# A second key table made on chip for the half units, presets of block one moved to weight places, and the second pair's loads issued later

## The chip, the cores and the metric

The kernel runs on one NeuronCore of a Trainium2 chip, in one launch. The metric is the device time of that core in microseconds (us); lower is better. The core has TensorE (PE, with its weight loads shown apart as PEld), VectorE (DVE), ScalarE (ACT), GpSimd (POOL) and SyncE (SP), which issues nearly all DMAs here.

## The reference

A linear attention with a decaying state, then two feed-forward layers one after the other. Batch 4, 8 heads, 768 steps, head width 48; so 3072 tokens of width 384, and a hidden width of 2048.

```python
for t in range(S):                       # attention, per batch and head
    cur = einsum('bhd,bhe->bhde', u * k[t], v[t])
    y[t] = einsum('bhd,bhde->bhe', r[t], state + cur)
    state = w * state + einsum('bhd,bhe->bhde', k[t], v[t])
x = y reshaped to (3072, 384)
h = x @ w_in;  x = (max(h, 0) + alpha * min(h, 0)) @ w_out        # layer A
h = x @ w_in2; x = (h * tanh(softplus(h))) @ w_out2               # layer B
```

## The kernel before

The sequence is cut into six blocks of 128 steps. A block holds all four batches. In block one each **unit** is one batch with its 128 steps (units 0 to 3, `B` = 4). From block two on a unit is half of a block's steps (64) of two batches ("half unit", units 4 to 23); two half units in a row make a **pair**, which shares one load of r and k. Inside a unit the recurrence is turned into matrix products: r and k are scaled by powers of the decay w (`prep_rk`, `prep_pair`, with the table `RK`), `scores` multiplies them (L337), a triangular mask copies the scores over a **preset** diagonal (`preset` on ACT, L319; `masked` on DVE, L341), and the result meets v (`attend0` L353, `batch` L369 and L390). The state `T` is updated from k times v (`states_first` L415, inside `batch` L383), with k scaled by a second table, `Kn`, whose row is the step and whose column is the feature (`prep_kn`, a multiplication on POOL, L310).

`Kn` comes from the inverse powers in `RK`: four ACT copies scale it by a power of w into a scratch tile (L251), four PE transposes turn it into the bank `acc2` (L252), two ACT copies bring it to SBUF (L255). That is written for 128 steps. The half units need the upper 64 rows of the table in both halves of the partitions, so `half_Kn` overwrites the lower half with the upper one by a DMA on SP's queue (L259), and `half_tables` makes the matching half identity and half mask on POOL (L177, L179). Both stand in the plan at the place -94.44, behind the multiplications of units 0 to 3, which need the full table.

After the attention of a block, layer A runs over its 512 tokens: 16 **slots** per block, one for each 128 columns of the hidden width. A slot multiplies x with a weight tile (`mA_h`, L156), applies the activation (ACT `m` L485, DVE `g` L487), splits the result into a high and a low part (ACT L82, DVE L85), and multiplies with the second half of the weight tile (`mA_out`, L517). In block one each weight tile f is also made just before its slot: a raw load (L102), two ACT scalings (L108, L109), a DVE join into `wj` (L114), a high part (ACT L82, or POOL L125 for odd f from 3 on) and a low part (DVE L85). Slot numbers start at 0 and run on; layer B follows when all of A is done.

The order of the work is written by hand. `at(place, work)` puts a piece of work at a place; all pieces are sorted by place, and the engines get them in that order. Places below -90 are the start, before slot 0; the dictionary `E` holds them by name. Each engine then works through its own list in order, so an instruction that waits holds up all that stand behind it on that engine. Loads stand in SP's list in the same way. A load also waits until one of eight completion slots is free, so that some eight loads of SP are under way at most.

Before any planned work SP gets the loads of units 0 to 3, the weights f = 0 to 2, both r and k loads of the first pair and the inputs of units 4 and 5, then f = 3, then `load_unit(B + 2)`: the eight r and k loads of the second pair (units 6 and 7) and the two of unit 6's r, k, v rows (`nat`); then f = 4 to 6. Weights f = 7 and on follow from the plan (at 0.4 and later). Tiles named `w8` to `w15` hold the inputs of units 0 to 3 until the weights with those numbers need the room; `wraw` has three buffers for raw weights. The preset tiles `A` (512 columns of fp32 for each of two halves) have two buffers in the attention's pool, for full and half units alike.

Of the kernel before, what the change touches and what calls it, by code (L numbers as in the profile page):

```python
# [36 lines left out]
PR = 112  # L37
# [26 lines left out]
def attention_and_two_ff(ctx: ExitStack, tc, rkT, nat, wT, ub, consts, w1, w2, alphaT, out):  # L64
    nc = tc.nc
    act, dve, pool, pe, dma = nc.scalar, nc.vector, nc.gpsimd, nc.tensor, nc.sync
    per = ctx.enter_context(tc.tile_pool(name="per", bufs=1))
# [114 lines left out]
    def by_seat(out, in_, *lead, by=(dma, dma)):  # L182

        for q, h, rows in ((0, 0, (0, 64, 0)), (1, 1, (48, 112, 48)), (0, 1, (0, 48, 64)), (1, 0, (64, 112, 0))):
            a, b, o = rows
            by[h].dma_start(out=out[(slice(o, o + b - a),) + lead + (slice(2 * q, 2 * q + 2),)],
                          in_=in_[(slice(a, b),) + lead + (slice(2 * h, 2 * h + 2),)])

    def load_unit(u):
        if u < B:  # L190
            f = NF - 2 * B + 2 * u
            rk = per.tile([PR, 2, NPR, C], F32, tag=f"w{f}", name=f"w{f}u")
            n = per.tile([128, 4, DM], F32, tag=f"w{f + 1}", name=f"w{f + 1}u")
            by_seat(rk, rkT[u], slice(None))
            dma.dma_start(out=n[:, 1:3], in_=nat[u, :, 1:3])
            inp[u] = (rk, n, n[:, 2])
            vz_t[u] = n[:, 3].rearrange("s (q c e) -> s q c e", q=2, c=KC)
            return
        j, bp, half = seat_of_unit(u)
        if half == 0:  # L200
            rk_t[j, bp] = [att.tile([PR, 2, NPR, C], F32, tag="rk", name="rk", bufs=4) for _ in range(2)]
            for i in range(2):
                by_seat(rk_t[j, bp][i], rkT[B * j + 2 * bp + i], slice(None))
        n = att.tile([128, 3, DM], F32, tag="nat", name="nat", bufs=3)
        for i in range(2):
            dma.dma_start(out=n[HALF[i]], in_=nat[B * j + 2 * bp + i, HALF[half]])
        inp[u] = (rk_t[j, bp], n, n[:, 2])

    RK = att.tile([PR, 2, NPR, C], F32, name="RK")
    uw = att.tile([PR, NPR, 2], F32, name="uw")  # L210
    w64 = att.tile([PR, NPR], F32, name="w64")
    w96 = att.tile([PR, NPR], F32, name="w96")
    Kn = att.tile([128, NPR, 2, D], F32, name="Kn")
    T = att.tile([PR, B, NPR, 64], F32, name="T")
    def tables():

# [27 lines left out]
        dve.tensor_copy(w64, sq[:, 1])  # L244
        mul(uw, uw, wide(wt, 2))

    def table_Kn():
        kw = new("m")[0:PR].rearrange("d (p s) -> d p s", p=NPR)
        t = bank("acc2")
        for p in range(NPR):  # L250
            act.activation(out=kw[:, p, :], in_=RK[:, 1, p, :], func=AF.Copy, scale=w96[:, p:p + 1])  # L251
            pe.transpose(t[:, p * C:p * C + PR], kw[:, p, :], ident[:PR, :PR])  # L252
        tv = t.rearrange("s (q r x) -> s q r x", q=2, r=2)
        for h, rows in enumerate(ROWS):
            act.activation(out=Kn[:, 2 * h:2 * h + 2].rearrange("s r q d -> s q r d"), in_=tv[:, :, :, rows], func=AF.Copy)  # L255

    def half_Kn():

        dma.dma_start(out=Kn[HALF[0]], in_=Kn[HALF[1]])  # L259

    w_stage = {0: "w4", 1: "w5", 2: "w6", 3: "w7", 7: "w9", 8: "w11", 9: "w13", 10: "w15"}

# [5 lines left out]
    A_t = {}  # L268
# [38 lines left out]

    def prep_kn(u):
        n = inp[u][1]
        pool.tensor_tensor(out=n[:, 1], in0=n[:, 1], in1=Kn.rearrange("s p a d -> s (p a d)"), op=ALU.mult)  # L310

    def preset(u, h):

        if h == 0:
            t = att.tile([128, 2, NPR, C], F32, tag="A", name="A", bufs=2)
            A_t[u] = t if u < B else t[:, 0].rearrange("s p t -> s (p t)").rearrange("s (h p t) -> s h p t", h=2, p=NPR)
        for j in range(NPR):
            p, q = HEAD[h, j]
            act.activation(out=A_t[u][:, h, j, :], in_=ident if u < B else id2, func=AF.Copy, scale=c_t[u][1][:, 2 * p + q, :])  # L319
# [324 lines left out]


    LAG = 2
    E = dict(warm=[-101.3, -99.45, -98.6, -98.1, -97.8, -96.05, -95.8, -93.45, -95.1, -94.8], Kn=[-97.9], rk=[-101.95, -100, -97.6, -95.7], c=[-100.45, -99.35, -96.95, -95.65], sc=[-99.7, -98.25, -96.5, -95.55], pad=[-99.95, -99.9, -97.75, -97], p=[-99.95, -99.2, -96.85, -95.6], m=[-98.95, -97, -96.2, -95.05], a=[-98.5, -96.05, -95.9, -94.95], hi=[-97.65, -95.4, -95.85, -94.65], lo=[-95.65, -94.15, -94.85, -94], kn=[-97.7, -96.05, -95.5, -94.45], st=[-95.3, 0.95], w=[-98.85, -96.4, -96, -95.25, -95, -94.85, -93.9, -93.9, -94.4, -0.5, 0.6, 0.85], u4=[-95.6, -94.95, 0.15, 0.1, 0.65, -94.35], u5=[0.2, 0.2, 2.25], half=[-94.44], p4=[-93.8, -93.7], m4=[0.75, 0.85])
    K = dict(scale=1.8, join=1.25, hi=1, lo=0.67, g=0.55, ghi=0.8, glo=1.1, t=1.25, x=0.7, pre0=0.65, pre1=0.7, m0=-0.25, m1=-0.9, c=-0.89, r0=-1.6, r1=-0.6, kn=0.7, c2=0.15)
    POOL_HI = range(3, NF, 2)
    AT = {B: 2} | {u: 4 * u - 15 for u in range(B + 1, NU)}  # L650
# [5 lines left out]
    def more_raw(upto):  # L656
        while w_next[0] < min(upto, NF):
            n = w_next[0]
            load_raw(0, n, w_stage.get(n, "wraw"))
            w_next[0] += 1  # L660
# [4 lines left out]
    def at(place, work, *args):  # L665
        plan.append((place, len(plan), work, args))
# [49 lines left out]
    with tc.manual_schedule():  # L716
# [3 lines left out]
        for h, i in HEAD:  # L720
            if i < 3 and i != 1:
                act.dma_start(out=uw[ROWS[h], i:i + 2, h],
                              in_=ub[0].rearrange("(h r q d) -> h q d r", h=2, r=2, q=2)[h, i // 2])
# [10 lines left out]
        more_raw(3)  # L734
        load_unit(B + 1)
        more_raw(4)
        load_unit(B + 2)
        more_raw(7)
        pool.memset(zz, 0.0)
        keep_warm(30)  # L740
# [2 lines left out]
        pool.memset(T, 0.0)  # L743
        tables()
        at(-100.5, dve.tensor_scalar, oma, al, -1.0, 1.0, ALU.mult, ALU.add)
        at(E["Kn"][0], table_Kn)
        for place in E["warm"]:
            at(place, keep_warm, 3)
        for u in range(B):
            for work, name in ((prep_rk, "rk"), (c_first, "c"), (pad_v, "pad"), (scores, "sc"),  # L750
                               (attend0, "a"), (x_first, "hi"), (x_first_lo, "lo")):
                at(E[name][u], work, u)
            for q in range(2):
                at(E["p"][u] + 0.01 * q, preset, u, q)
                at(E["m"][u] + 0.01 * q, masked, u, q)
            at(E["kn"][u], prep_kn, u)
        at(E["half"][0], half_Kn)
        at(E["half"][0], half_tables)
        at(E["st"][0], states_first, 0)
        at(E["st"][1], states_first, 2)  # L760
        for f in range(3):
# [18 lines left out]
        for f in range(NF):  # L780
            s = 16 + 4 * f
# [18 lines left out]
        for n in range(0, NB + LAG_B, 2):  # L800
# [7 lines left out]
            for m in pair:  # L808
# [78 lines left out]
```

## Time and profile before

| what | value |
|---|---|
| runs of the kernel before | 1450.11, 913.66, 916.17 us; median 916.17 us |
| the profiled execution, its own time | 912.67 us |
| its span in the profile | 910.9 us, so 1.8 us lie around it |
| mean granted TensorE clock | 0.984 of full speed |
| busy in the span | PE 97%, PEld 84%, DVE 70%, ACT 68%, POOL 10% |
| chain of work that ended last | PE 86%, DVE 3%, ACT 2% of the span |

The profile is of one execution. Engines' shares are of the whole span; the parts of the span differ, and the rows below are therefore cut to stretches. Times in rows are us from the span's start. A row of the timeline gives the start, the length, the engine, the line, the operation, and in brackets how long the engine had stood idle and what ended that. Matmuls overlap, so that the length of several together is not the sum. The clock column of a window is the granted TensorE clock, 1.00 for 2.4 GHz and 0.50 for 1.2 GHz.

### The profile page before, as it was taken

Reading aid. Unit: us, or ns where it says so; the run is one execution under the profiler, and the core shown is the slowest. Engines: PE = TensorE matmul, PEld = TensorE weight load, DVE = VectorE, ACT = ScalarE, POOL = GpSimd, SP = SyncE. Lnnn points to the kernel's source line nnn. Section 1 sums busy time; section 2 is a strip of 40 time slices with the busy share of each in tenths; the row PEclk is TensorE's granted clock in tenths of the full one; section 3 lists DMA queues with packets and bytes.
Section 4 is the critical chain, followed back from the end, with each engine's and each line's share of the span. In section 5 each row is a group of like instructions: output and inputs, shape, how many; then the busy total and the mean of one; then the engine's idle time right before and its main releaser. Section 6 shows DMA issues by size and latency. Waiting matters only on the chain.

```text
span 910.9 us, 17108 instructions
## 1 busy us (share of the span) xinstructions
PE 883.9 (97%) x6684; PEld 761.3 (84%) x6684; DVE 636.3 (70%) x1025; ACT 623.2 (68%) x1193; POOL 90.2 (10%) x112
## 2 busy tenths in 40 slices
PE   9859999999999999999999999999999999999998
PEld 8747878887887887888888898998999999989997
DVE  5639876565665665644565687787787787787876
ACT  4746744554444544454454798898898898898985
POOL 1322231211112111110001100000000000000000
PEclk9879999999999999999999999999999999999999
DMA  7974433435434444311442200200100200100000
GB/s 224 235 271 148 135 103 123 136 108 155 144 113 130 149 138 145 128 63 62 162 133 69 105 1 1 70 1 1 70 1 0 70 1 1 36 1 1 35 1 35
DMA packets 34672, 79.79 MB, mean 88 GB/s; under 512 B 5728, under 2 KB 21792, under 8 KB 34592
## 3 DMA queue, kind: packets, MB, share of 16 engines
q1 hardware_dynamic: 34000, 78.70, 27.8%
q8 instruction: 52, 0.85, 0.4%
q14 instruction: 28, 0.23, 0.1%
q10 hardware_dynamic: 592, 0.00, 0.0%
HBM read 60.89 MB, written 15.73 MB: 84 GB/s over the span
## 4 chain that ended last, share of the span: by engine, by line
PE 86%; DVE 3%; ACT 2%; issue 1%; DMA 1%; POOL 0%; SPq 0%; DVEq 0%; ACTq 0%; POOLq 0%
PE h L156 40%; PE acc L517 20%; PE acc L625 10%; PE sc L625 7%; PE yt L625 3%; PE sc L337 1%; PE sc L383 1%; PE yt L390 1%; PE h L369 1%; DVE rk L280 1%; PE yt L369 1%; DMA x<-y 1%; POOL w L125 0%; SPq L458 0%; ACT ghi L82 0%
## 5 line engine op out<-in xcount | busy, mean ns | idle before, releaser
L156 PE MATMUL h<-x,w 128*128 128x512 f32 x1728 | 419.7, 392 | 6.2 <-DMA x<-y 2.7
L156 PEld LDWEIGHTS h<-x,w 128*128 128x128 f32 x1728 | 323.4, 188 | 76.1 <-issue 5.6
L517 PE MATMUL acc<-ghi,w 128*128 128x512 f32 x516 | 178.1, 399 | 0.0
L485 ACT ACTIVATE m<-h 128x512 f32<-128x512 f32 x96 | 57.3, 597 | 105.0 <-PE h L156 105.0
L517 PEld LDWEIGHTS acc<-ghi,w 128*128 128x128 f32 x516 | 98.5, 191 | 22.4
L487 DVE SCALAR_TENSOR_TENSOR g<-m,oma,h 128x512 f32<-128x512 f32 x96 | 71.5, 745 | 64.2 <-ACT m L485 63.9
L82 ACT ACTIVATE ghi<-g 128x512 fp32r<-128x512 f32 x86 | 54.3, 631 | 77.4 <-PE acc L517 55.3
L517 PE MATMUL acc<-glo,w 128*128 128x512 f32 x258 | 102.2, 396 | 0.0
L85 DVE TENSOR_TENSOR glo<-g,ghi 128x512 fp32r<-128x512 f32 x86 | 60.8, 707 | 57.7 <-ACT ghi L82 57.7
L625 PE MATMUL acc<-w,ghiB 128*128 128x384 f32 x384 | 98.0, 336 | 0.0
L573 DVE SCALAR_TENSOR_TENSOR a<-ghi,h 128x512 f32<-128x512 f32 x96 | 66.0, 687 | 36.1 <-ACT ghi L570 28.6
L573 DVE SCALAR_TENSOR_TENSOR g<-s,c 128x512 f32<-128x512 f32 x96 | 66.3, 690 | 22.0 <-ACT s L570 19.0
L82 ACT ACTIVATE ghiB<-g 128x512 fp32r<-128x512 f32 x106 | 65.8, 621 | 18.5 <-DVE g L573 8.0
L85 DVE TENSOR_TENSOR gloB<-g,ghiB 128x512 fp32r<-128x512 f32 x106 | 72.6, 685 | 7.8 <-ACT ghiB L82 7.8
L581 ACT ACTIVATE m<-h 128x512 f32<-128x512 f32 x96 | 56.0, 584 | 27.9 <-PE h L156 27.9
L570 ACT ACTIVATE ghi<-m,half 128x512 f32<-128x512 f32 x96 | 69.6, 725 | 3.2
L625 PEld LDWEIGHTS acc<-w,ghiB 128*128 128x128 f32 x384 | 69.7, 188 | 1.3
L570 ACT ACTIVATE glo<-ghi,m 128x512 f32<-128x512 f32 x96 | 68.0, 708 | 0.1
L570 ACT ACTIVATE s<-s,m 128x512 f32<-128x512 f32 x96 | 68.0, 709 | 0.0
L570 ACT ACTIVATE s<-glo,m 128x512 f32<-128x512 f32 x96 | 68.0, 709 | 0.0
L573 DVE SCALAR_TENSOR_TENSOR b<-ghi,a 128x512 f32<-128x512 f32 x96 | 67.4, 702 | 0.1
L573 DVE SCALAR_TENSOR_TENSOR c<-glo,b 128x512 f32<-128x512 f32 x96 | 65.7, 684 | 0.0
(174 smaller groups left out, 1193.7 us busy)
## 6 DMA issues: line engine op xcount, KB each, us to landing
wrawr<-in_w SPq DMA_DIRECT2D x24, 768.0 KB, 4.6
nat<-in_nat SPq DMA_DIRECT2D x40, 288.0 KB, 4.3
w2d<-wj SPq DMA_DIRECT2D x16, 384.0 KB, 2.7
wraw<-w2d SPq DMA_DIRECT2D x16, 384.0 KB, 3.0
rk<-in_rkT SPq DMA_DIRECT2D x40, 128.0 KB, 3.0
x2d<-xo SPq DMA_DIRECT2D x6, 768.0 KB, 4.0
x<-x2d SPq DMA_DIRECT2D x6, 768.0 KB, 4.3
out<-oo SPq DMA_DIRECT2D x24, 192.0 KB, 1.9
```

The source lines that it names most:

```text
L82: act.activation(out=hi, in_=src, func=AF.Copy)
L85: eng.tensor_tensor(out=lo, in0=src, in1=hi.bitcast(F32), op=ALU.subtract)
L156: pe.matmul(h, w_in(layer, f, a, c), x[:, b, c, :], start=(k == 0), stop=(k == 3 * KC - 1))
L280: dve.tensor_tensor(out=rk, in0=rk, in1=w.unsqueeze(2).to_broadcast([PR, 2 * NPR, 2, HC]), op=ALU.mult)
L369: pe.matmul(y[i][64 * q:64 * q + 64, p * HC:(p + 1) * HC], T[ROWS[h], 2 * bp + i, k, :], pair[i][ROWS[h], 0, k, t], start=(r == 0 and not ...
L485: act.activation(out=m, in_=hA[s], func=AF.Relu, scale=-1.0)
L487: dve.scalar_tensor_tensor(out=g, in0=m, scalar=oma[:, f:f + 1], in1=hA.pop(s), op0=ALU.mult, op1=ALU.add)
L517: pe.matmul(acc[0][c], w_out(0, f, a)[:, c * 128:(c + 1) * 128], g[b], start=(f == 0 and k == 0), stop=(f == NF - 1 and k == 2))
L570: act.activation(out=out, in_=in_, func=AF.Square, scale=scale, bias=fin[bias])
L573: dve.scalar_tensor_tensor(out=out, in0=in0, scalar=scalar, in1=in1, op0=op0, op1=ALU.mult)
L581: act.activation(out=bnew("t", n), in_=v["h", n], func=AF.Tanh, scale=0.5)
L625: pe.matmul(acc[1][t][:, :DM], g[a][:, t * C:(t + 1) * C], w_out(1, f, b), start=(f == 0 and k == 0), stop=(f == NF - 1 and k == 2))
```

## The change

Three things are done.

- `Kn` gets a leading index of two. `table_Kn(0)` makes the full table at place -97.9 as before; `table_Kn(1)` makes one for the half units at -95.25: the four scaling copies read the upper 64 steps twice, so that the transposes leave them in both halves of the partitions. `prep_kn` takes table 1 for half units. `half_Kn` and its DMA go. In `E`, `Kn=[-97.9]` becomes `Kn=[-97.9, -95.25]`; no other place in it changes.
- The preset tiles of block one lie in the places of the weight tiles f = 2 and 3; the half units' presets have their own tile `Ah`, half as large, in two buffers.
- `load_unit(B + 2)` moves from the list written ahead of the plan to the plan, at place 1.5.

```diff
-    Kn = att.tile([128, NPR, 2, D], F32, name="Kn")
+    Kn = att.tile([128, 2, NPR, 2, D], F32, name="Kn")
...
-    def table_Kn():
+    def table_Kn(i):
+
         kw = new("m")[0:PR].rearrange("d (p s) -> d p s", p=NPR)
         t = bank("acc2")
         for p in range(NPR):
-            act.activation(out=kw[:, p, :], in_=RK[:, 1, p, :], func=AF.Copy, scale=w96[:, p:p + 1])
+            if i:
+                act.activation(out=kw[:, p, :].rearrange("d (h s) -> d h s", h=2), func=AF.Copy, scale=w96[:, p:p + 1],
+                               in_=RK[:, 1, p, HC:].unsqueeze(1).to_broadcast([PR, 2, HC]))
+            else:
+                act.activation(out=kw[:, p, :], in_=RK[:, 1, p, :], func=AF.Copy, scale=w96[:, p:p + 1])
             pe.transpose(t[:, p * C:p * C + PR], kw[:, p, :], ident[:PR, :PR])
         tv = t.rearrange("s (q r x) -> s q r x", q=2, r=2)
         for h, rows in enumerate(ROWS):
-            act.activation(out=Kn[:, 2 * h:2 * h + 2].rearrange("s r q d -> s q r d"), in_=tv[:, :, :, rows], func=AF.Copy)
-
-    def half_Kn():
-
-        dma.dma_start(out=Kn[HALF[0]], in_=Kn[HALF[1]])
+            act.activation(out=Kn[:, i, 2 * h:2 * h + 2].rearrange("s r q d -> s q r d"), in_=tv[:, :, :, rows], func=AF.Copy)
...
-        pool.tensor_tensor(out=n[:, 1], in0=n[:, 1], in1=Kn.rearrange("s p a d -> s (p a d)"), op=ALU.mult)
+        pool.tensor_tensor(out=n[:, 1], in0=n[:, 1], in1=Kn[:, u >= B].rearrange("s p a d -> s (p a d)"), op=ALU.mult)
...
-            t = att.tile([128, 2, NPR, C], F32, tag="A", name="A", bufs=2)
-            A_t[u] = t if u < B else t[:, 0].rearrange("s p t -> s (p t)").rearrange("s (h p t) -> s h p t", h=2, p=NPR)
+            A_t[u] = (per.tile([128, 2, NPR, C], F32, tag=f"w{2 + u % 2}", name="A") if u < B
+                      else att.tile([128, 2, NPR, HC], F32, tag="Ah", name="Ah", bufs=2))
...
-        load_unit(B + 2)
...
-        at(E["Kn"][0], table_Kn)
+        for i in range(2):
+            at(E["Kn"][i], table_Kn, i)
...
-        at(E["half"][0], half_Kn)
         at(E["half"][0], half_tables)
+        at(1.5, load_unit, B + 2)
```

On ACT, near the end of block one's attention, the list of the kernel before has the copies of the first state `T` and then the scalings of weight f = 1 (`w5r`):

```order
L82 ACTIVATE x<-acc_295 128x3x128
L417 ACTIVATE T<-acc_490 48x8x48 x2
L108 ACTIVATE w5r<-w5r 128x768
L109 ACTIVATE w5r<-w5r 128x768
L82 ACTIVATE x<-h 128x3x128
```

In the changed kernel the same place reads:

```order
L82 ACTIVATE x<-acc_282 128x3x128
L418 ACTIVATE T<-acc_477 48x8x48 x2
L253 ACTIVATE m<-RK,w_97 112x128 x4
L260 ACTIVATE Kn<-acc_497 128x2x2x48 x2
L108 ACTIVATE w5r<-w5r 128x768
L109 ACTIVATE w5r<-w5r 128x768
L82 ACTIVATE x<-h 128x3x128
```

Six ACT instructions have come in ahead of weight f = 1 and of the split of unit 3's result. On PE the same step puts four transposes between the states of units 0 and 1 (L415 before, L416 after) and the product of unit 3 (L353, L354). PE of the kernel before:

```order
L415 MATMUL acc_490<-w9u 48x48 x8
L415 MATMUL acc_490<-w11u 48x48 x8
L469 MATMUL acc_510<-ghi 128x128 x3
L353 MATMUL h<-A,w15u 64x128 x6
L353 MATMUL h<-A,w15u 48x128 x6
```

PE of the changed kernel:

```order
L416 MATMUL acc_477<-w9u 48x48 x8
L416 MATMUL acc_477<-w11u 48x48 x8
L257 MATMUL acc_497<-cst,m 128x112 x4
L470 MATMUL acc_509<-ghi 128x128 x3
L354 MATMUL h<-A,w15u 64x128 x6
L354 MATMUL h<-A,w15u 48x128 x6
```

The transposes stand ahead of unit 3's product; the L469 (L470) matmuls are ones on zeros that keep TensorE busy. On SP, from the raw load of f = 2 (`w6r`) on, the kernel before has:

```order
L102 DMA w6r<-in_w 128x1536
L206 DMA nat<-in_nat 64x1152 x2
L102 DMA w7r<-in_w 128x1536
L186 DMA rk<-in_rkT 64x2x256 x2
L186 DMA rk<-in_rkT 48x2x256 x2
L186 DMA rk<-in_rkT 64x2x256 x2
L186 DMA rk<-in_rkT 48x2x256 x2
L206 DMA nat<-in_nat 64x1152 x2
L102 DMA wrawr<-in_w 128x1536 x3
L259 DMA Kn<-Kn 64x384
L102 DMA w9r<-in_w 128x1536
L102 DMA w11r<-in_w 128x1536
```

The changed kernel has there:

```order
L102 DMA w6r<-in_w 128x1536
L206 DMA nat<-in_nat 64x1152 x2
L102 DMA w7r<-in_w 128x1536
L102 DMA wrawr<-in_w 128x1536 x3
L102 DMA w9r<-in_w 128x1536
L102 DMA w11r<-in_w 128x1536
L186 DMA rk<-in_rkT 64x2x256 x2
L186 DMA rk<-in_rkT 48x2x256 x2
L186 DMA rk<-in_rkT 64x2x256 x2
L186 DMA rk<-in_rkT 48x2x256 x2
L206 DMA nat<-in_nat 64x1152 x2
L102 DMA w13r<-in_w 128x1536
```

The second pair's ten loads stand behind the raw weights f = 4 to 8 instead of ahead of them, and the table's copy is gone. The lists of POOL and DVE keep their order.

## Rows read from the trace of the kernel before

**Rows 1.** Page, part 1: busy time, share of the span and instructions.
```profile
PE 883.9 (97%) x6684; PEld 761.3 (84%) x6684; DVE 636.3 (70%) x1025; ACT 623.2 (68%) x1193; POOL 90.2 (10%) x112
```
**Rows 2.** Waits, 40 to 85 us: who waited for whom, total, times, longest.
```profile
POOL nat L310 <- DMA Kn<-Kn: 17.1, 1, 17.1
```
**Rows 3.** Timeline, 45 to 63 us, the first half unit's batch (slots 0 to 2).
```profile
45.20 0.51 SPq L259 DMA_DIRECT2D Kn<-Kn  x1
...
52.47 0.58 ACT L485 ACTIVATE m<-h 128x512 f32<-128x512 f32 x1
56.01 0.99 POOL L310 TENSOR_TENSOR nat<-nat,Kn 128x384 f32<-128x384 f32 x1 [17.10 <-DMA Kn<-Kn]
...
57.06 1.11 PE L383 MATMUL sc<-nat 64*64 64x48 f32 x32 [6.68 <-POOL nat L310]
...
60.04 0.83 POOL L125 CAST w<-wj 128x768 fp32r<-128x768 f32 x1
...
61.78 0.74 DVE L487 SCALAR_TENSOR_TENSOR g<-m,oma,h 128x512 f32<-128x512 f32 x1
...
62.46 0.79 PE L517 MATMUL acc<-ghi,w 128*128 128x512 f32 x1
```
**Rows 4.** Windows: stretch, length, busy PE, PEld, DVE, ACT, POOL; clock; DMA share; GB/s.
```profile
50.39:60.97 10.58, 1.11 (x32) 0.95 (x32) 1.05 (x3) 3.19 (x7) 4.75 (x6) 0.62 0.87 336
64.15:67.36 3.21, 3.21 (x10) 2.50 (x10) 0.87 (x2) 0.83 (x3) 0.00 (x0) 0.63 0.97 255
84.36:99.30 14.94, 14.94 (x84) 12.13 (x86) 12.67 (x18) 10.02 (x15) 4.61 (x4) 1.00 0.50 143
61.78:79.02 17.24, 15.83 (x100) 12.20 (x91) 14.36 (x23) 8.84 (x19) 4.36 (x5) 0.86 0.53 172
```
**Rows 5.** Timeline, 79 to 82 us: the second half unit's batch (slot 3's second product).
```profile
79.08 0.69 PE L337 MATMUL sc<-rk 48*64 48x64 f32 x32 [0.77 <-DVE A L341]
...
79.59 0.63 PE L383 MATMUL sc<-nat 64*64 64x48 f32 x32
...
81.42 0.79 PE L517 MATMUL acc<-ghi,w 128*128 128x512 f32 x1
```
**Rows 6.** Timeline, 18 to 21 us: ACT's part of the full table.
```profile
18.84 1.26 ACT L251 ACTIVATE m<-RK,w 112x128 f32<-112x128 f32 x4
...
20.51 0.55 ACT L255 ACTIVATE Kn<-acc 128x192 f32<-128x192 f32 x2 [0.41 <-PE acc L252]
```
**Rows 7.** Timeline, 35 to 44 us: where the second table is put in, and behind it.
```profile
35.07 0.97 ACT L417 ACTIVATE T<-acc 48x384 f32<-48x384 f32 x2
...
42.40 1.22 DVE L280 TENSOR_TENSOR rk<-rk,RK 112x1024 f32<-112x1024 f32 x1
...
43.67 0.69 PE L337 MATMUL sc<-rk 48*64 48x64 f32 x32 [1.31 <-DVE rk L280]
```
**Rows 8.** Windows around the full table and the start of slot 0, columns as in 4.
```profile
17.00:22.00 5.00, 4.24 (x53) 3.23 (x53) 3.55 (x5) 4.21 (x12) 0.86 (x1) 1.00 1.06 280
22.40:28.50 6.10, 6.10 (x61) 5.51 (x62) 3.58 (x6) 3.65 (x11) 1.78 (x2) 0.50 1.01 235
38.00:45.00 7.00, 4.61 (x78) 3.54 (x79) 6.34 (x10) 6.38 (x15) 0.87 (x1) 1.00 0.86 202
```
**Rows 9.** Timeline, 69 to 77 us: the second pair's scalings, alone and beside POOL.
```profile
69.37 1.22 DVE L280 TENSOR_TENSOR rk<-rk,RK 112x1024 f32<-112x1024 f32 x1
...
74.46 1.60 POOL L302 TENSOR_TENSOR nat<-nat 128x384 f32<-128x384 f32 x1
...
75.11 2.02 DVE L280 TENSOR_TENSOR rk<-rk,RK 112x1024 f32<-112x1024 f32 x1
```
**Rows 10.** Timeline of SP's queue, 30 to 49 us: issue times of loads.
```profile
30.63 11.59 SPq L186 DMA_DIRECT2D rk<-in_rkT  x8
...
47.58 0.49 SPq L102 DMA_DIRECT2D w11r<-in_w  x1
```
**Rows 11.** DMA issues, 30 to 60 us: count, size, us to landing.
```profile
w11r<-in_w SPq DMA_DIRECT2D x1, 768.0 KB, 11.7
```

More of the change, by code (lines that the diff above doesn't have):

```diff
@@ L646, in attention_and_two_ff @@
     LAG = 2
-    E = dict(warm=[-101.3, -99.45, -98.6, -98.1, -97.8, -96.05, -95.8, -93.45, -95.1, -94.8], Kn=[-97.9], rk=[-101.95, -100, -97.6, -95.7], c=[-100.45, -99.35, -96.95, -95.65], sc=[-99.7, -98.25, -96.5, -95.55], pad=[-99.95, -99.9, -97.75, -97], p=[-99.95, -99.2, -96.85, -95.6], m=[-98.95, -97, -96.2, -95.05], a=[-98.5, -96.05, -95.9, -94.95], hi=[-97.65, -95.4, -95.85, -94.65], lo=[-95.65, -94.15, -94.85, -94], kn=[-97.7, -96.05, -95.5, -94.45], st=[-95.3, 0.95], w=[-98.85, -96.4, -96, -95.25, -95, -94.85, -93.9, -93.9, -94.4, -0.5, 0.6, 0.85], u4=[-95.6, -94.95, 0.15, 0.1, 0.65, -94.35], u5=[0.2, 0.2, 2.25], half=[-94.44], p4=[-93.8, -93.7], m4=[0.75, 0.85])
+    E = dict(warm=[-101.3, -99.45, -98.6, -98.1, -97.8, -96.05, -95.8, -93.45, -95.1, -94.8], Kn=[-97.9, -95.25], rk=[-101.95, -100, -97.6, -95.7], c=[-100.45, -99.35, -96.95, -95.65], sc=[-99.7, -98.25, -96.5, -95.55], pad=[-99.95, -99.9, -97.75, -97], p=[-99.95, -99.2, -96.85, -95.6], m=[-98.95, -97, -96.2, -95.05], a=[-98.5, -96.05, -95.9, -94.95], hi=[-97.65, -95.4, -95.85, -94.65], lo=[-95.65, -94.15, -94.85, -94], kn=[-97.7, -96.05, -95.5, -94.45], st=[-95.3, 0.95], w=[-98.85, -96.4, -96, -95.25, -95, -94.85, -93.9, -93.9, -94.4, -0.5, 0.6, 0.85], u4=[-95.6, -94.95, 0.15, 0.1, 0.65, -94.35], u5=[0.2, 0.2, 2.25], half=[-94.44], p4=[-93.8, -93.7], m4=[0.75, 0.85])
     K = dict(scale=1.8, join=1.25, hi=1, lo=0.67, g=0.55, ghi=0.8, glo=1.1, t=1.25, x=0.7, pre0=0.65, pre1=0.7, m0=-0.25, m1=-0.9, c=-0.89, r0=-1.6, r1=-0.6, kn=0.7, c2=0.15)
```

## The prediction

> **What bounds the kernel now.** I read the page's busy times first: PE is busy 883.9 us of the 910.9 us span [rows 1]. So nearly all of the span is matmul work, and a change that adds no matmul work of size can only gain where PE stands still. The waits of the first 85 us come next. The longest is one wait of POOL: 17.1 us for the DMA that copies half of `Kn` over the other half [rows 2]. The timeline shows what hangs on it. SP issues the copy at 45.20, and the multiplication that needs it starts at 56.01 [rows 3]; the 96 KB arrive 10.8 us after their issue, since the queue is full: a weight issued 2.4 us later took 11.7 us [rows 10, 11]. PE's state product L383 needs the multiplied k and waits 6.68 us, from 50.38 to 57.06 [rows 3]. Then POOL works off what it could not do before: the input of unit 5, the cast of weight 3 at 60.04, and the memset of `T` behind that. PE reaches the first second product (L517, slot 0) only at 62.46 [rows 3]. In 50.39 to 60.97 PE is busy 1.11 us of 10.58 and its mean clock is 0.62 of full speed [rows 4]. Last I looked at how far this reaches. From 84.36 to 99.30 PE is busy the whole 14.94 us at full clock [rows 4], so time that is won before that carries on to the end. Between the stall and that point DVE decides: it is busy 14.36 us of 17.24 from slot 2's `g` (61.78) to 79.02 [rows 4], when its second masking lets PE start the scores of the next unit (79.08, after 0.77 us of waiting) [rows 5].
>
> **The stall that goes.** Without the copy, the multiplication waits for the second table on ACT alone, which by the terms below is there at 36.04 + 2.22 = 38.3. PE then goes from the scores' end at 50.38 straight into L383. The second batch shows the way from there to L517 without that stall: 79.59 to 81.42, 1.83 us [rows 5]. What is late next is the memset of `T`, which stands on POOL behind the cast of weight 3; that cast takes 0.83 us [rows 3] and waits for weight 3's join on DVE. I take 0.5 us for it (bounds 0 and 0.83, the whole cast; a part of it lies beside L383). L517 would start at 50.38 + 1.83 + 0.5 = 52.7, against 62.46: 9.75 us earlier, less a delay S from the new table.
>
> **What DVE lets through.** That gain has to pass DVE. Ahead of slot 2's `g` on DVE stand unit 5's sum and the low part of weight 3, which waited for POOL; the other input of `g`, ACT's `m`, was ready at 52.47 + 0.58 = 53.05 [rows 3]. In the changed kernel it starts there (plus S) instead of at 61.78, 8.7 us earlier. From there to the masking DVE needs at least its busy time, 14.36 us, and at most the old 17.24 [rows 4]. Of the idle 2.88 us, 3.21 - 0.87 = 2.34 lie in 64.15 to 67.36, when the mean clock was 0.63 [rows 4] and DVE waited, over ACT, for a buffer that PE's product gives back; with PE at full clock I leave 0.7 of all of it. So the masking ends at 53.05 + 14.36 + 0.7 = 68.1 plus S, against 79.02: 10.9 us earlier less S, with bounds 8.7 (all idle stays) and 11.6 (none). This is the term I use; the 9.75 of PE's own way, plus what the half clock cost there, is about as much.
>
> **The new table (S).** On ACT: the first table took 1.26 us for four scalings, 0.41 us of waiting for the transposes and 0.55 us for two copies [rows 6], 2.22 us in all. It is put in behind the copies of `T`, which end at 36.04 [rows 7]. ACT is busy 6.38 of 7.00 us from 38 to 45 [rows 8], so nothing hides it: the weight scalings, the join on DVE, the pair's scaling at 42.40 and the scores at 43.67, which wait for that scaling (1.31 us) [rows 7], all slide by it. The four transposes on PE stand ahead of unit 3's product and hold it until about 37.5; its split on ACT stands behind the table and two weight scalings, so PE's delay is covered. I take 2.2 us (bounds 1.2, if slack before slot 1 takes a part, and 2.2).
>
> **POOL's work moves beside DVE's.** Four POOL multiplications of some 1.0 us (two with `Kn`, two for unit 5) leave a stretch where DVE was busy 1.05 of 10.58 us [rows 4] for 39 to 45 us, where it is busy 6.34 of 7.00 [rows 8]. The trace shows what such a meeting costs: the scaling of a pair takes 1.22 us alone and 2.02 us beside a POOL multiplication, 0.80 us more [rows 9]. Bounds: 0, and 4 x 0.80 = 3.2 us. I take 1.0, since the table also leaves DVE about 2 us of waiting for ACT, in which POOL can work. The Trainium skill (SBUF — State Buffer, "Who interferes with whom") has a rule that speaks against the change here: a DVE instruction with two inputs in SBUF and a GpSimd instruction that reads SBUF exclude each other, and the later one waits for the whole of the earlier. The row agrees: POOL's work ends at 74.46 + 1.60 = 76.06, and 1.22 us later is 77.28, near the scaling's end at 77.13. By the rule the join, the weight's low part, the next join and the scaling can each be held once, the upper bound; by the row alone only the scaling is sure.
>
> **The clock.** The first table's sparse matmuls were followed by a fall: PE was busy 4.24 of 5.00 us in 17 to 22, and from 22.4 to 28.5 the granted clock was 0.50 (1.2 GHz) for 6.10 us. In 38 to 45 PE was busy 4.61 of 7.00 and the clock stayed at 1.00 [rows 8]. The second table makes that stretch sparser. Bounds: 0, and half of a 6.10 us stretch, 3.05 us; I take 0, after the nearer stretch.
>
> **The loads.** The second pair's ten loads now follow five weights of 768 KB. Before, everything up to the weight f = 8 had landed at 47.58 + 11.7 = 59.3 [rows 10, 11]; the changed queue carries the same bytes up to that point less 96 KB, in another order, so I expect the pair by 59.3. Its first reader is DVE's scaling at 69.37 [rows 9], which moves to 61.7. Weights f = 4 and on come earlier than before, which hides nothing that was waited for. Cost 0, with 2.4 us in hand. Below 0 nothing is seen, since no wait of DVE for the weights stands in that stretch.
>
> **Presets.** The same copies with other addresses: the weight tiles 2 and 3 are first written after unit 2's and 3's products, weight 3 by the cast at 60.04 [rows 3], some 52 then; unit 3's product ends near 40. Cost 0, both ways.
>
> **Sum.** S = 2.2 + 1.0 = 3.2. Gain 10.9 - 3.2 = 7.7 us. The profiled execution took 912.67 us, so 905.0 us (span 903.2). The median of the runs shown, 916.17, lies 3.5 us above that execution, so against the median the same kernel would look 1.2% faster. 2% of it, 18.3 us, is about what a measurement of this kernel can tell from no change.
>
> **Rivals.**
> - *The table gives back most of it.* Both open costs at their upper ends: S = 2.2 + 3.2 + 3.05 = 8.45, gain 2.4, 910.2 us. For: DVE and ACT have no room in 38 to 45 [rows 8], and the clock did fall behind the first table. Against: it did not fall in the stretch that is nearest. The rule from the SBUF page belongs to this case.
> - *More is won.* S at 1.2 and no idle on DVE: 11.6 - 1.2 = 10.4, 902.3 us; or another half-clock stretch goes too, near 900.
> - *The second pair comes too late (slower).* Place: DVE's first scaling of unit 6, behind which stand slot 3's `g`, the joins and the masking that PE waits for. For: its eight loads alone took 11.59 us to issue [rows 10], since a load waits for the one eight before it, and now those are weights. Price: one us for each us after 61.7. It takes back the gain if they land at 69.4; at 72.4 the time is 912.67 + 3.0 = 915.7. Against: they would have to land 13 us after the same bytes had landed before.
> - *The wait was another's.* If POOL's first multiplication, or the cast behind it, waits for something else as long, the gain is 0 and S is paid: 912.67 + 3.2 = 915.9. Against: unit 4's other inputs were multiplied on POOL long before, and in the changed lists that instruction waits for ACT and POOL alone.
>
> **How the numbers follow.** Forecast, 902 to 908 with 905.0: 0.68. The table gives most back, 908 to 913: 0.17. More is won, below 902: 0.08. Late pair: 0.04. Another's wait: 0.03. The range takes in both bounds and the 2.5 us by which the two runs 913.66 and 916.17 differ: 899 to 914. To pass 2% the time must be below 897.8 or above 934.5. No row gives 15 us, and no rival costs 18: 0.03 faster, 0.95 same, 0.02 slower.
>
> **What would show it.** In the changed profile the row of POOL's wait for `Kn` is gone; L383 starts within 0.2 us of the scores' end, near 53.6; the first L517 near 55.9; the scores after the second masking near 71.3 instead of 79.08; the clock holds 1.00 from 50 to 65. The table shows as 2.2 us on ACT at 36. It is wrong if DVE's scaling of unit 6 waits for a DMA, if the clock is 0.50 within 37 to 50, or if DVE's rows in 39 to 45 are 0.8 us longer several times over; and wrong at the root if POOL still waits past 50.

## Result and profile after

The changed kernel takes 904.13 us (median of four: 904.27, 905.25, 904.00, 901.86). The kernel before, run beside it, took 913.66, 916.17 and 911.77; a fourth execution of it, 1450.11, is left out of the comparison as disturbed. The ratio is 0.989 [0.9852, 0.9928]: about 1% faster, inside the 2% that counts as the same. The forecast was 905.0 in 899 to 914. The profiled execution took 904.27 us with a span of 902.5; that of before took 912.67 with 910.9. So one execution against the other it is 8.4 us less, where 7.7 were forecast.

Behind the function that makes the table, line numbers are one higher than before: L383 is now L384, L517 is L518. The table's own lines L251, L252 and L255 are now L253, L257 and L260. The page of the changed kernel, part 1, answers to [rows 1]:

```profile
PE 882.0 (98%) x6688; PEld 759.4 (84%) x6688; DVE 638.5 (71%) x1025; ACT 624.6 (69%) x1199; POOL 89.5 (10%) x112
```

PE is as busy as before. What went is idle time. The waits of 40 to 85 us, to hold against [rows 2] (who waited for whom: total, times, longest):

```profile
POOL w L125 <- DVE wj L114: 11.9, 1, 11.9
...
PE sc L338 <- DVE rk L281: 2.8, 1, 2.8
```

No row has a DMA as releaser any more, and none has `Kn`. POOL's longest wait is now for the join of weight 3. Its length means little: POOL had worked off everything else by then. The timeline, 31 to 75 us, which answers to [rows 3, 5, 7]:

```profile
32.64 0.97 ACT L418 ACTIVATE T<-acc 48x384 f32<-48x384 f32 x2
...
33.62 1.28 ACT L253 ACTIVATE m<-RK,w 112x128 f32<-112x128 f32 x4
...
35.44 0.55 ACT L260 ACTIVATE Kn<-acc 128x192 f32<-128x192 f32 x2 [0.54 <-PE acc L257]
...
37.70 1.73 POOL L311 TENSOR_TENSOR nat<-nat,Kn 128x384 f32<-128x384 f32 x1
...
38.89 0.49 ACT L82 ACTIVATE x<-h 128x384 fp32r<-128x384 f32 x1 [1.32 <-PE h L354]
...
41.75 1.79 DVE L85 TENSOR_TENSOR w<-wj,w 128x768 fp32r<-128x768 f32 x1 [1.77 <-ACT w L82]
...
45.60 1.13 PE L338 MATMUL sc<-rk 48*64 48x64 f32 x32 [2.83 <-DVE rk L281]
...
54.39 0.65 PE L338 MATMUL sc<-rk 48*64 48x64 f32 x32
54.58 1.15 POOL L125 CAST w<-wj 128x768 fp32r<-128x768 f32 x1 [11.86 <-DVE wj L114]
54.86 0.63 PE L384 MATMUL sc<-nat 64*64 64x48 f32 x32
...
56.64 0.74 DVE L488 SCALAR_TENSOR_TENSOR g<-m,oma,h 128x512 f32<-128x512 f32 x1
56.68 0.50 PE L518 MATMUL acc<-ghi,w 128*128 128x512 f32 x1
...
61.73 1.22 DVE L281 TENSOR_TENSOR rk<-rk,RK 112x1024 f32<-112x1024 f32 x1
...
71.46 0.69 PE L338 MATMUL sc<-rk 48*64 48x64 f32 x32 [0.77 <-DVE Ah L342]
...
74.10 0.79 PE L518 MATMUL acc<-ghi,w 128*128 128x512 f32 x1
```

The second table stands on ACT from 33.62 to 35.99, 2.37 us. The multiplication of k with it starts at 37.70 instead of 56.01. The state product L384 starts 0.47 us behind unit 5's scores without waiting, where L383 waited 6.68 us. Slot 0's second product starts at 56.68 instead of 62.46, the scores behind the second masking at 71.46 instead of 79.08, slot 3's second product at 74.10 instead of 81.42.

The windows (columns as in [rows 4]; the third stretch is the same time as there, the fourth is the same place of the program, from slot 2's `g` to the end of the second masking, and the fifth answers to the last full stretch there, 84.36 to 99.30):

```profile
34.80:38.00 3.20, 3.20 (x22) 2.86 (x24) 1.11 (x3) 2.23 (x5) 3.02 (x6) 0.50 1.01 230
44.90:51.60 6.70, 6.00 (x72) 5.12 (x73) 3.52 (x6) 3.69 (x6) 0.00 (x0) 0.50 1.05 312
50.39:60.97 10.58, 10.24 (x161) 8.26 (x160) 7.78 (x16) 8.37 (x21) 1.20 (x2) 0.94 0.87 233
56.64:71.41 14.77, 13.33 (x78) 10.31 (x70) 14.32 (x23) 9.48 (x22) 4.38 (x5) 1.00 0.77 246
76.95:91.00 14.05, 14.05 (x63) 11.63 (x62) 11.86 (x16) 9.48 (x14) 4.59 (x4) 1.00 0.51 148
```

In 50.39 to 60.97 PE is now busy 10.24 of 10.58 us (1.11 before). The first two rows show what the forecast did not have: PE's clock fell to 1.2 GHz twice, the second time from about unit 4's scores to the end of slot 1's first product.

### The profile page after: what moved, and what is told of

It is laid out like the page before. It is cut to its first block, busy times and chain, and to the rows that moved or that the text cites. A ratio compares the mean times of both kernels' runs of the same rounds, so it can differ in the third digit from the quotient of the medians.

```text
span 902.5 us, 17129 instructions
## 1 busy us (share of the span) xinstructions
PE 882.0 (98%) x6688; PEld 759.4 (84%) x6688; DVE 638.5 (71%) x1025; ACT 624.6 (69%) x1199; POOL 89.5 (10%) x112
## 4 chain that ended last, share of the span: by engine, by line
PE 85%; DVE 2%; ACT 2%; DMA 2%; issue 1%; SPq 1%; POOL 0%; ACTq 0%; DVEq 0%; POOLq 0%
PE h L156 40%; PE acc L518 19%; PE acc L626 10%; PE sc L626 7%; PE yt L626 3%; PE sc L338 1%; DMA x<-y 1%; DMA w15r<-in_w 1%; PE sc L384 1%; PE h L370 1%; PE yt L391 1%; DVE rk L281 1%; PE yt L370 1%; SPq L459 0%; DVE wj L114 0%
## 5 line engine op out<-in xcount | busy, mean ns | idle before, releaser
L518 PE MATMUL acc<-ghi,w 128*128 128x512 f32 x516 | 176.0, 395 | 0.0
L518 PEld LDWEIGHTS acc<-ghi,w 128*128 128x128 f32 x516 | 97.2, 188 | 21.9
L518 PE MATMUL acc<-glo,w 128*128 128x512 f32 x258 | 101.1, 392 | 0.0
L574 DVE SCALAR_TENSOR_TENSOR g<-s,c 128x512 f32<-128x512 f32 x96 | 66.3, 691 | 22.4 <-ACT s L571 19.1
```

What stands on the lines that cost most here:

```text
L518: pe.matmul(acc[0][c], w_out(0, f, a)[:, c * 128:(c + 1) * 128], g[b], start=(f == 0 and k == 0), stop=(f == NF - 1 and k == 2))
L574: dve.scalar_tensor_tensor(out=out, in0=in0, scalar=scalar, in1=in1, op0=op0, op1=ALU.mult)
```

## Experiments

The theory to be tested: POOL's wait for the copy was the stall; the table on chip removes it and costs S on ACT and DVE; the loads' place and the presets cost and give nothing. The main rival for the changed time: the moved loads make the gain, by letting the copy or the weights come earlier. All ratios are to the kernel before, run beside each kernel. The places that the text compares, in us from the start of the span of one profiled execution each ("clock" is the mean granted clock of that execution):

| kernel | `T` copies end | unit 4's scores | unit 5's scores | scores after the second masking | span | clock |
|---|---|---|---|---|---|---|
| before | 36.04 | 43.67 | 49.74 | 79.08 | 910.9 | 0.984 |
| changed | 33.61 | 45.60 | 54.39 | 71.46 | 902.5 | 0.992 |
| e1 table without loads | 33.50 | 45.40 | 51.47 | 69.53 | 900.6 | 0.998 |
| e2 loads without table | 33.52 | 42.39 | 48.46 | 71.65 | 904.4 | 0.994 |
| e3 presets alone | 33.90 | 42.34 | 49.51 | 78.54 | 910.0 | 0.992 |
| e5 changed, kept warm | 33.49 | 45.28 | 51.35 | 68.83 | 899.2 | 1.000 |
| e10 e5 less unit 5's POOL work | 33.25 | 43.59 | 49.65 | 67.15 | 900.1 | 0.996 |
| e11 e5 with the old loads | 33.31 | 44.67 | 50.73 | 70.02 | 900.4 | 1.000 |

**Which part of the change does it: e1, e2, e3.** e1 is the changed kernel with the second pair's loads at their old place:

```diff
+        load_unit(B + 2)
         more_raw(4)
...
-        at(1.5, load_unit, B + 2)
```

> The changed kernel with the second pair's ten loads put back ahead of the weights f = 4 to 6; table and presets stay as changed. Theory (the stall was the wait for the copy alone, the loads' place is worth little): POOL's long wait stays away, weight f = 4 is first scaled near 51 to 53 us as in the changed kernel, and the time is within 2 us of the changed kernel's (ratio to before 0.987 to 0.991). Rival (the queue's order carries part of the gain): f = 4 to 6 land as late as before while the slots come 8 us earlier, ACT or DVE waits for a raw weight by 2 us or more, and the ratio is 0.993 or above.

Measured: 903.22 us, ratio 0.9886 [0.9867, 0.9904], the same as the changed kernel's 0.989. The loads add nothing to the table that a whole time shows.

e2 is the kernel before with the loads moved and all else, the copy too, left as it was:

```diff
-        load_unit(B + 2)
         more_raw(4)
...
         at(E["half"][0], half_Kn)
+        at(1.5, load_unit, B + 2)
```

> The kernel before with only the second pair's loads moved behind the weights; the table for half units is still copied by the DMA, no second table is made. Theory (the copy was late because of what stood ahead of it in the queue, and the table's own cost is S): the copy is issued near 38 us and lands by 47, POOL's wait ends before PE needs the product near 50, PE does not stall, and as S of 2 to 4 us is not paid the ratio is 0.984 to 0.989, no slower than the changed kernel. Rival (the copy is the fault wherever its loads stand): it lands after 52, PE still waits 2 us or more for POOL, ratio 0.993 or above.

Measured: 906.74 us, ratio 0.9924 [0.9901, 0.9948]. That is about two thirds of e1's gain, where the prediction had put the loads at nothing. It lies between what this run's theory expected (0.989 at most) and its rival (0.993 or above). The timeline of e2:

```profile
35.72 1.72 POOL L310 TENSOR_TENSOR w15u<-w15u,Kn 128x384 f32<-128x384 f32 x1
...
36.91 0.91 ACT L108 ACTIVATE w6r<-w6r 128x768 f32<-128x768 f32 x1 [1.09 <-DMA w6r<-in_w]
...
37.47 0.51 SPq L259 DMA_DIRECT2D Kn<-Kn  x1
...
49.13 1.27 POOL L310 TENSOR_TENSOR nat<-nat,Kn 128x384 f32<-128x384 f32 x1 [10.94 <-DMA Kn<-Kn]
...
50.45 0.68 PE L383 MATMUL sc<-nat 64*64 64x48 f32 x32 [1.35 <-POOL nat L310]
...
53.45 0.82 POOL L125 CAST w<-wj 128x768 fp32r<-128x768 f32 x1
...
54.37 0.36 PE L369 MATMUL yt<-rk,T 48*64 48x64 f32 x1 [3.23 <-POOL T L373]
```

and its DMA issues (count, size, us from issue to landing):

```profile
Kn<-Kn SPq DMA_DIRECT2D x1, 96.0 KB, 11.5
```

Ten loads no longer stand ahead of the copy on SP, so it is issued at 37.47 instead of 45.20 [rows 3], as soon as POOL's last multiplication with the full table ends (35.72 + 1.72 = 37.44). I had expected it to have landed by 47 us; it still takes 11.5 us to arrive (10.7 before). But POOL's multiplication now starts at 49.13 instead of 56.01, and PE's wait in L383 shrinks from 6.68 to 1.35 us. What POOL could not do before piles up behind it: the memset of `T`, which stands behind the cast at 53.45, holds PE another 3.23 us. So e2 pays for the shorter stall, but owes no S; its unit 5 scores come at 48.46, earliest of all here. The stall had two cures: take the copy away, or let it be issued sooner. The table gives all of the gain, the earlier issue about two thirds of it, and the loads' new place on top of the table adds nothing that a whole time shows.

e3 is the kernel before with the presets alone changed:

```diff
-            t = att.tile([128, 2, NPR, C], F32, tag="A", name="A", bufs=2)
...
+            A_t[u] = (per.tile([128, 2, NPR, C], F32, tag=f"w{2 + u % 2}", name="A") if u < B
+                      else att.tile([128, 2, NPR, HC], F32, tag="Ah", name="Ah", bufs=2))
```

> The kernel before with only the presets of block one in the places of weights 2 and 3 and the half units' presets in tiles of their own. Theory: no time, ratio 0.997 to 1.003, with the 17 us wait of POOL as before. Rival: presets of the half units that no longer share a buffer with units 2 and 3 come earlier, or weight 2's high part waits for a preset's readers; either would show as 2 us or more one way.

Measured over ten executions: 912.43 us, ratio 1.000 [0.9983, 1.0017]. The presets are worth nothing that this can show (0.17%, 1.6 us, either way), and its waits of 40 to 85 us have the row of [rows 2] as before:

```profile
POOL nat L310 <- DMA Kn<-Kn: 15.0, 1, 15.0
```

**The clock: e5.** The changed kernel with 8 and 9 more of the small filler matmuls (`keep_warm`) that it already has at ten other places:

```diff
         for place in E["warm"]:
             at(place, keep_warm, 3)
+        at(-95.26, keep_warm, 8)
+        at(0.645, keep_warm, 9)
```

> The changed kernel with matmuls on zeros added in the two gaps that its PE shows before the clock falls: 8 calls ahead of the second table's transposes (2.5 us idle) and 9 ahead of unit 4's scores (2.8 us idle). Theory (the fall to 0.50 in 45 to 51.6 us slows the products of slots 1 and 2 and so costs about 3 us): the clock stays at 1.00 from 34 to 60, the scores of unit 5 start near 51.5 instead of 54.4, ratio to before 0.984 to 0.987. Rival (those products are waited for by nothing that is late, or the clock falls somewhere else instead): 0.7 us or less, ratio 0.988 to 0.990.

Measured: 901.27 us (900.95 to 901.78), ratio 0.9863 [0.9832, 0.9895]. Its windows over the two stretches in which the changed kernel's clock had fallen:

```profile
34.80:38.00 3.20, 3.20 (x38) 2.83 (x37) 0.76 (x2) 2.81 (x6) 3.14 (x5) 1.00 0.99 297
44.90:51.60 6.70, 6.32 (x116) 5.19 (x120) 4.60 (x8) 4.47 (x8) 0.00 (x0) 1.00 1.01 274
```

At full clock the second stretch holds 116 matmul records instead of 72. Unit 5's scores come at 51.35 instead of 54.39, 3.04 us earlier, and the scores behind the second masking 2.63 us earlier. The span is 3.3 us shorter and the median 2.9. So the clock term of S, which I had put at 0, was about 3 us in the profiled execution. Nearly all of it is the second fall: from unit 4's scores to unit 5's it takes 8.79 us in the changed kernel, and 6.06 or 6.07 in all others of the table but e3.

It is not in every execution: e1, whose program is the same up to its loads, had only one short fall, 0.50 from about 34 to 37, and its unit 5 scores came at 51.47. What sets a fall off was not found. Before the second fall PE was busy 4.71 of 6.90 us (38.00 to 44.90); in e2 it was busy 4.62 us in the same stretch, and no fall followed.

**POOL beside DVE: e7 and e10.** Both leave out unit 5's three POOL multiplications (its two bonus products and its k scaling); e7 is the changed kernel without them, e10 is e5 without them:

```diff
     def prep_c(u):
         n = inp[u][1]
         c_t[u] = n[:, 0].rearrange("s (h d) -> s h d", h=H), new_c(u)
+        if u == B + 1:
+            return
...
     def prep_kn(u):
+        if u == B + 1:
+            return
         n = inp[u][1]
```

> The changed kernel without the three POOL multiplications for unit 5 (its u-weighted k and its k scaling are left out, so unit 5's share of the output is not the reference's); all else stands. It measures what POOL's work beside DVE costs. Theory (it holds DVE's two-input instructions, my term of 1.0 us): the low part of weight 1 takes 0.95 us instead of 1.79, unit 4's scores start 0.8 to 1.6 us earlier after the end of the T copies, ratio 0.986 to 0.9885. Rival (ACT and PE set the path there): 0.4 us or less at the scores, ratio 0.9885 to 0.990.

Measured: 901.94 us, ratio 0.987 [0.9843, 0.9896]. As a whole time, and at the scores, it is inconclusive: its clock fell over the very rows to be compared. The window, clock in the third column from the right:

```profile
33.00:41.00 8.00, 6.99 (x41) 5.87 (x42) 4.05 (x7) 5.49 (x12) 6.06 (x8) 0.57 1.03 271
```

The instruction itself came out as expected. The low part of weight 1 takes 0.96 us, where it takes 1.79 in the changed kernel (41.75):

```profile
42.23 0.96 DVE L85 TENSOR_TENSOR w<-wj,w 128x768 fp32r<-128x768 f32 x1 [1.75 <-ACT w L82]
```

> The kernel with the added matmuls on zeros at two places (whose clock stayed at 1.00), without POOL's three multiplications for unit 5, whose share of the output is again not the reference's. It measures POOL beside DVE without the clock's noise. There the weight's low part took 1.41 us, the join 1.76 and the pair's scaling 2.02 instead of 0.95, 0.95 and 1.22, 2.0 us more. Theory (this delay is on the path): unit 4's scores start 1.4 to 2.1 us earlier after the T copies' end (there 45.28 for 33.49), ratio 0.9835 to 0.9855 against 0.9863. Rival (it is covered): 0.5 us or less, ratio 0.9855 to 0.987.

Measured: 900.7 us, ratio 0.9872 [0.9837, 0.9908]. As a whole time this can't be told from e5. The rows can. DVE around the pair's scaling in e5, with POOL beside it:

```profile
39.78 1.01 POOL L302 TENSOR_TENSOR nat<-nat,ubt 128x384 f32<-128x384 f32 x1
...
40.20 1.41 DVE L85 TENSOR_TENSOR w<-wj,w 128x768 fp32r<-128x768 f32 x1 [0.45 <-ACT w L82]
...
40.87 1.60 POOL L303 TENSOR_TENSOR nat<-nat 128x384 f32<-128x384 f32 x1
...
41.53 1.76 DVE L114 SCALAR_TENSOR_TENSOR wj<-w6r 128x768 uint32<-128x768 uint32 x1
...
42.55 1.60 POOL L311 TENSOR_TENSOR nat<-nat,Kn 128x384 f32<-128x384 f32 x1
...
43.21 2.02 DVE L281 TENSOR_TENSOR rk<-rk,RK 112x1024 f32<-112x1024 f32 x1
```

and in e10, with the nine fillers of PE:

```profile
39.98 0.96 DVE L85 TENSOR_TENSOR w<-wj,w 128x768 fp32r<-128x768 f32 x1 [0.48 <-ACT w L82]
40.85 0.95 DVE L114 SCALAR_TENSOR_TENSOR wj<-w6r 128x768 uint32<-128x768 uint32 x1
...
41.49 2.17 PE L474 MATMUL acc<-ghi 128*128 128x128 f32 x18
...
41.72 1.22 DVE L281 TENSOR_TENSOR rk<-rk,RK 112x1024 f32<-112x1024 f32 x1
```

Three instructions in a row are longer by 0.45, 0.81 and 0.80 us while POOL multiplies. [rows 9] shows one such; the trace of before had a second just ahead of it, which I had not read (POOL works at 73.37 to 74.38 there):

```profile
73.44 1.75 DVE L85 TENSOR_TENSOR w<-wj,w 128x768 fp32r<-128x768 f32 x1 [0.35 <-POOL w L125]
```

Unit 4's scores come 1.69 us earlier in e10 than in e5, 1.45 us counted from the end of the `T` copies. DVE gave more than that: the pair's scaling ends at 42.94 instead of 45.23, 2.29 us earlier, or 2.05 counted from the `T` copies. In e10, though, PE is busy with the fillers until 43.66, and the scores start at 43.59. So the price of POOL beside DVE at full clock is 1.45 to 2.05 us, where I took 1.0. In e5 each of the three ends close to where the POOL multiplication that it meets ends, plus its own length alone: 40.79 + 0.96 = 41.75 (measured 41.61), 42.47 + 0.95 = 43.42 (43.29), 44.15 + 1.22 = 45.37 (45.23). It is what the Trainium skill's rule cited in the prediction (SBUF — State Buffer, "Who interferes with whom") would do, and the join shows the same lengthening.

**The table earlier, and warm: e4, e6, e12.** The changed kernel with the second table ahead of the state products instead of behind them (e4), and the same with nine filler matmuls (e6; e12 is e6 once more, in more executions):

```diff
 E = dict(
...
-Kn=[-97.9, -95.25],
+Kn=[-97.9, -95.895],
...
+        at(0.645, keep_warm, 9)
```

> The changed kernel with the second table made earlier, at -95.895, ahead of the split of unit 2's result, where ACT of the changed kernel stands idle 1.8 and 1.2 us. Theory (the table's 2.2 us on ACT at 34 to 36 us lie on the path): ACT's weight f = 1 begins 1.5 to 2.2 us sooner, the scores behind slot 1 come 1.5 to 3 us sooner, ratio 0.985 to 0.988. Rival (the path there is set by POOL's multiplications beside DVE or by the clock, not by ACT): no more than 0.7 us, ratio 0.988 to 0.991.

Measured: 901.62 us, ratio 0.9865 [0.9846, 0.9885]. Its profile had clock falls of its own (about 23 to 29 and 46 to 49), so what the place alone is worth can't be read from it.

> The changed kernel with the second table at -95.895 and 9 calls of matmuls on zeros ahead of unit 4's scores. Theory (table's time on ACT and the clock's fall behind slot 0 are separate costs, 2 us and up to 3): the second fall of the early-table kernel (47 to 49.1) goes, ratio 0.982 to 0.9855. Rival (the early table alone has what there is): ratio 0.985 to 0.988.

Measured: 900.13 us, ratio 0.985 [0.9821, 0.9879], clock 1.000, unit 5's scores at 51.06 against 51.35 in e5. The table's place gives 0.3 us there. The `T` copies now end 1.05 us later (34.54), and behind them ACT waits 0.44 us for the raw weight f = 2.

> The same kernel as the early table with 9 calls of matmuls on zeros ahead of unit 4's scores, timed in more rounds, to see whether it beats the changed kernel clear of the spread. Theory (clock held, part of S gone): median 899.5 to 901.5 us, spread under 4 us, ratio to before 0.984 to 0.987. Rival (its first four runs were lucky with the clock): median above 902.5, ratio 0.988 or above.

Measured over six executions: 900.4 us (899.63 to 904.29), ratio 0.9875 [0.9843, 0.9908]. The median is where the theory had it; the spread (4.66 us) and the ratio are a little above. By the medians it beats both kernels, the one before by 13 us and the changed one by some 4 us. Against the kernel before that is clear. Against the changed kernel it is not: the two intervals overlap.

**The loads once more, at full clock: e8, e9, e11.** e8 is e4 with the loads at the old place, e9 is e8 with fillers at three places (3, 3 and 8), e11 is e5 with the loads at the old place (its edit is that of e1).

> The changed kernel with the second table at -95.895 and the second pair's loads back ahead of weights f = 4 to 6. Theory (the loads' place is worth nothing once the copy is gone, the table's place 2 us): ratio 0.985 to 0.988, as with the early table alone. Rival (with the slots still earlier, weights f = 4 to 6 now come too late): ACT waits 1 us or more for a raw weight, ratio 0.988 or above.

Measured: 903.88 us, ratio 0.9889 [0.9842, 0.9936], with a wide spread: 899.03 at a mean clock of 1.000, the other three 903.67 to 908.58 at 0.989 to 0.994. The ratio is the rival's, and in the profiled execution, the fastest, ACT does wait 1.1 us for a raw weight. So the clock alone is not shown to make the spread.

> The kernel of the early table and old loads (its four runs spread from 899.03 to 908.58 us) with matmuls on zeros in three gaps: 3 calls ahead of unit 3's product, 3 ahead of slot 0, 8 ahead of unit 4's scores. Theory (the spread is the clock, which falls in some executions, and S is gone): clock 1.00 in all runs up to 60 us, spread under 2.5 us, ratio to before 0.981 to 0.985. Rival (the spread comes from raw weights that land late behind the second pair's loads): the spread stays above 4 us and the ratio at 0.986 or above.

Measured: 902.09 us (899.83 to 905.47), ratio 0.9892 [0.9858, 0.9927]. This expectation missed. The clock was 1.000 in four of the six executions (0.998 and 0.992 in the others), the profiled one took 901.61, and the gain over e6 that I expected did not come. Spread (5.6 us) and ratio are the rival's, but in the profiled execution ACT waits only 0.6 us for a raw weight, so the rival's cause is not shown either. The four at 1.000 still differ by 2.7 us.

> The kernel with the added matmuls on zeros at two places and the second pair's loads back ahead of weights f = 4 to 6. With the clock out of the way it compares the loads' two places. Theory (worth nothing): ratio 0.985 to 0.9875, no wait for a raw weight or for r, k of 1 us or more. Rival: old place dearer by 2 us or more, ratio 0.9885 or above, with a DMA wait on ACT or DVE.

Measured: 902.7 us, ratio 0.989 [0.9855, 0.9925], at clock 1.000, against e5's 901.27. ACT in e11:

```profile
52.96 0.94 ACT L108 ACTIVATE wrawr<-wrawr 128x768 f32<-128x768 f32 x1 [1.95 <-DMA wrawr<-in_w]
```

With the loads ahead of the weights, ACT waits 1.95 us for a raw weight, as the rival had it. From unit 5's scores to those behind the second masking it takes 19.3 us (50.73 to 70.02) instead of 17.5 in e5 (51.35 to 68.83), and the span is 1.2 us longer. So the loads' new place is worth 1 to 2 us, but only where the slots come early enough to need it; the medians' intervals are too wide to show it as a whole time.

## Why the prediction was right, and where it was not

**The stall** held at every place. POOL's wait for `Kn` went with the copy, L384 follows the scores at once, and e3, which keeps the copy, keeps the stall. The root was put too narrowly, though. I read the wait as the price of a copy in a full queue. e2 shows that the copy's place in SP's list was as much its cause: 7.7 us earlier issued, 6.9 us earlier used. The 3.23 us that PE waits for the memset in e2 are what I had allowed 0.5 us for in the changed kernel; there POOL is idle ahead of the cast, and PE's next product waits only 0.34 us.

**What DVE lets through** held: 14.77 us from slot 2's `g` to the masking, 14.32 of it busy, where I took 14.36 + 0.7 = 15.06. PE is busy throughout from 76.95, as it was from 84.36 in [rows 4], so the gain carries on. The scores behind the second masking are 7.62 us earlier. The span gained 0.8 us more than that. The kernel before had a clock fall later on that the changed one's execution did not have (its 120 to 130 us had a mean clock of 0.83, the changed kernel's 1.00). But e2, at 1.00 there too, is 7.43 us ahead of the kernel before at that masking and 6.5 in the span. So where the 0.8 us come from stays open.

**S is the term that failed**, in all of its three parts, and other errors offset it. Forecast and measured, for unit 5's scores:

| term | forecast | measured | from |
|---|---|---|---|
| start, as in the trace of before | 49.74 | 49.74 | |
| that execution's own early clock fall | not seen as a term | -1.28 | before to e2 |
| table on ACT, and POOL beside DVE | 2.2 + 1.0 = 3.2 | 2.89 | e2 to e5; of it POOL 1.45 to 2.05 (e5 to e10) |
| clock | 0 | 3.04 | e5 to the changed kernel |
| unit 5's scores | 52.94 | 54.39 | |

Each is a difference of two profiled executions, and e3, which I would expect to equal e2 at this place, is 1.05 us later (ACT's presets for unit 4 wait 2.03 us there for POOL's copies of the half tables); so no term is surer than about 1 us. The sum of table and POOL was nearly right, by offsetting parts. POOL cost 0.45 to 1.05 us more than the 1.0. ACT's table cost 0.8 to 1.4 on the path instead of 2.2, though it is 2.37 long; my lower bound of 1.2 was nearer. e2 shows what took a part of it: without the table ACT waits 1.09 us for the raw weight f = 2 (36.91), and with it there is no such wait.

In the changed kernel's own execution the first clock fall shifts this. There ACT waits 1.32 us for unit 3's product (38.89), which I had called covered, and it starts on weight f = 2 1.55 us later than in e5 (39.28 for 37.73). But DVE then meets only one of POOL's multiplications on the way to unit 4's scores, and loses 0.83 us to it instead of 2.06. So of the 1.55 us of the first fall 0.32 is left at unit 4's scores (45.60 for 45.28); the second fall costs 2.72 behind them.

The wrong step is "Bounds: 0, and half of a 6.10 us stretch, 3.05 us; I take 0, after the nearer stretch". What was measured, 3.04 us, is near the upper bound. I had written that the forecast would be wrong if the clock was 0.50 within 37 to 50, and it was, up to 38.0 and from 44.9 on. (The sign for POOL, several DVE rows in 39 to 45 longer by 0.8 us, did not show in that profile: one row is.) That the total came out all the same is luck, in two parts. The first is that the execution of before carried a fall of its own at 22.4 to 28.5 [rows 8], which later ones (e1, e2, e3, the changed kernel's) did not: the `T` copies ended at 36.04 there and at 33.5 to 33.9 in these. In the kernel before such a fall costs next to nothing at the end, since POOL waits for the copy anyway: e3 without it has its span 0.9 us shorter and its L383 still at 57.27. I had counted 36.04 as the program's; it was that execution's. The second part is told under the loads.

**The loads.** Cost 0 held: DVE's scaling of unit 6 (61.73; I expected 61.7) waits for no DMA, and the rival of the late pair is dead. "Weights f = 4 and on come earlier than before, which hides nothing that was waited for" was wrong. The trace of before had such a wait, and I had not read it:

```profile
50.93 0.88 ACT L108 ACTIVATE wrawr<-wrawr 128x768 f32<-128x768 f32 x1 [0.92 <-DMA wrawr<-in_w]
```

In the changed kernel ACT does not wait there (L108 at 54.15). That helps explain why slot 2's `g` starts 2.25 us behind unit 5's scores (54.39 to 56.64), where its input was there 3.31 us behind them before (49.74 to 53.05). These 1.06 us and the 0.29 us of the DVE stretch took back all but 0.1 of the 1.45 us by which the scores were late: the second masking ended at 71.41, forecast 71.3. e1 (0.67 us of that wait) and e11 (1.95 us) show the wait come back with the old place; in e11, which differs from e5 in the loads alone, slot 2's `g` starts 4.46 us behind unit 5's scores instead of 2.68.

**Presets:** 0, as far as e3 can show.

## What to carry to other kernels

When an engine waits for a small DMA, look at what stands ahead of it in the issuing queue before taking the DMA away: moving ten loads behind it gave two thirds of what replacing it gave. A profiled execution holds its own clock falls; before a start time is used as a base, see whether the clock was 1.00 up to it, and price the term at both levels. Work that frees one engine early lands beside another's: count every row there that has grown, not the one that the old trace happened to show.

## What was not expected of the hardware

- The clock falls came in some executions and not in others of the same program. Executions of e8 went from 899.03 us at a mean clock of 1.000 to 908.58 at 0.989. Seventeen filler matmuls kept the clock at 1.00 throughout in e5's profile, but two of e5's four executions have mean clocks of 0.996 and 0.998. e12, which has nine and the early table, still has a fall in its profile: the mean clock in 68 to 72 us is 0.58.
- Instructions of DVE are held by POOL's one after the other. Three in a row lost 0.45, 0.81 and 0.80 us in e5.
- The 96 KB copy within SBUF took over 10 us to arrive whether it was issued at 45.20 or at 37.47 us: 10.7 us in the kernel before, 11.5 in e2. With the weights under way it was hardly faster than a load of eight times its size (11.7 us, [rows 11]).
